# Splitting the final range checks of a list-scheduled attention kernel, moving them ahead of the last residual adds, and re-tuning the scheduler with it

## The chip, the cores and the metric

The kernel runs on one core of one Trainium2 chip. Time is device microseconds (us) of one execution of the whole program. Runs are only compared with runs of the same rounds on the same chip, unless the text says otherwise. e1 to e4 ran on one chip and e5 to e12 on another; the record doesn't name the chip of the comparison with the changed kernel. Engines: PE is TensorE (matmuls), PEld its weight loads, DVE is VectorE, ACT is ScalarE, POOL is GpSimd, SP is SyncE (transfers).

## The reference, cut to what matters

Four layers work on x of 2048 rows by 512 columns, in bf16: A, B, A, B, each as `x + f(layernorm(x))`. A is attention of 32 heads over eight dilated neighbours of each position. B is full attention in which 32 query heads share one key and value head, and it is most of the work:

```python
scores = jnp.einsum("bhqd,bkd->bhqk", q, k) * (Dh ** -0.5)   # 32 heads x 2048 x 2048
p = _softmax(scores, axis=-1)
o = jnp.einsum("bhqk,bkd->bhqd", p, v)
return o.transpose(0, 2, 1, 3).reshape(B, S, H * Dh) @ wo    # then x + this
...
x = A_x
x = x + _A_ref(_layernorm(x), ...)      # and B, and A, and B again
```

## The kernel before

The softmax is computed without subtracting a row's maximum. ScalarE takes some of the exponentials as a real `exp`; VectorE and GpSimd take the rest in pieces: VectorE copies a tile of scores out as 16-bit integers ("t"), and "passes" on integers then shift it ("i"), one on VectorE and others on GpSimd. This is only right while sums and reciprocals stay in range, so running sums (`chk_a`, `chk_b`, and two wide ones in the tile `oncA`) are compared with limits at the end: flags are made with `is_lt`, a minimum is taken, one matmul counts partitions that are good, and the verdict `chk_bad` decides whether a slow, safe program runs after all. In all runs here it doesn't.

The order of instructions on each engine is settled when the program is built, by a list scheduler with planned durations. It takes the candidate with the lowest key. Priorities are nanoseconds added to the planned start, so "LATER" is half a microsecond:

```python
AGE = 0.034
FIRST, SOON, LATER = -1000.0, -500.0, 500.0
SPAN, ACTIVE = 3413.0, 0.74
SLACK, PATIENCE = 798.0, 70.6
...
            if e in op.port:                      # VectorE/GpSimd work that declares `port`
                s = max(s, self.port)
            s = self.pe_start(op.mode, op.sub, s) if e == "pe" else max(s, self.now[e])
            if s < FAR:
                key = s + op.prio - AGE * (s - op.ready)
                if s + op.engs[e] + SWITCH > due + SLACK and s - op.ready < PATIENCE:
                    key = max(key, due + 1.0)
...
    def keep_awake(self, until):                  # called before each planned TensorE operation
        ...
        active = sum(b - max(a, old) for a, b in self.array_busy if b > a)
        t = min(gap, ACTIVE * SPAN - active)      # matmuls on zeros, if the plan is less busy than ACTIVE
```

The last block of the last layer ends in `close_tail(a, evac)`, called for its two halves a = 0 and 1. `evac` is VectorE's copy of a finished sum of attention products (`X <- o`); the copy of the second half ends the stream of attention tiles. Then come sums (`dn`), a logarithm and an exponential on ScalarE for reciprocals (`rec`), two normalisations on VectorE (`ons`), four output products, four residual adds and the checks:

```python
    def close_tail(self, a, evac):
        ...
        if a == 0:
            self.on0, self.seen = ons[0], sees
            return

        def most(op):       # five flags and one reduction of 1344 elements
            for i in self.checks.flag_most(self.i[0][:].rearrange("p r c -> p (r c)").bitcast(BF16)):
                self.chain("dve", i)

        y, adds = {}, []
        self.op("dve", 2300.0, most, [evac, *self.seen, *sees], prio=LATER)
        ...                 # four products begin, two to each score buffer
            m = self.op("pe", MM, end, [ons[qi // 2], begun[qi]], solid=True)
            adds.append(self.op("dve", 599.0, lambda op, qi=qi: self.add_y(l, qc, qi, y[qi]), [m], prio=SOON))

        def last(op):       # flag and minimum of the last reciprocals, count, chk_bad
            ...
        rec.used(self.op("dve", 1500.0, last, adds))
```

Of the kernel before, what the change touches and what calls it, by code (L numbers as in the profile page):

```python
# [435 lines left out]
SLACK, PATIENCE = 798.0, 70.6  # L436
# [179 lines left out]
class Stream:  # L616

    GROUP = 4
    BIAS = {"act": -50.0, "act2": 1946.7, "vec": 438.1, "pv": 246.6, "pv_in": 177.5, "batch": 17, "few": 19.9,
            "copy": 1.6, "pass": 76.2, "lag": -1045.1, "both": 216.8, "next": 634.6, "late": 31.8, "open": 54.2,  # L620
# [217 lines left out]
class Checks:  # L838
# [4 lines left out]
    def __init__(self, nc, pool):  # L843
        self.nc, self.pool = nc, pool
        self.a = pool.tile([128, 256], F32, name="chk_a")
        self.b = pool.tile([128, 2, 32], F32, name="chk_b")
        self.t = None
        self.blank = [nc.vector.memset(x[:], 0.0) for x in (self.a, self.b)]
# [12 lines left out]
    def flag_most(self, ok):  # L861
        nc, v = self.nc, self.nc.vector
        self.ok, self.mb = ok, self.pool.tile([128, 2], BF16, name="chk_mb")
        out = [v.tensor_scalar(out=ok[:, at:at + n], in0=x, scalar1=lim, scalar2=None, op0=ALU.is_lt)
               for at, n, x, lim in ((0, 256, self.a[:], self.LOG_A ** 2), (256, 32, self.b[:, 0, :], self.SUM_B),
                                     (288, 32, self.b[:, 1, :], self.REC_B), (320, 512, self.t[:, 0, :], self.SUM_B),
                                     (832, 512, self.t[:, 1, :], self.REC_B))]
        return [*out, v.tensor_reduce(out=self.mb[:, 0:1], in_=ok[:, 0:1344], axis=AX.X, op=ALU.min)]

    def flag_last(self, recips):  # L870
        v, ok = self.nc.vector, self.ok[:, 1344:1856]
        return [v.tensor_scalar(out=ok, in0=recips, scalar1=self.REC_B, scalar2=None, op0=ALU.is_lt),
                v.tensor_reduce(out=self.mb[:, 1:2], in_=ok, axis=AX.X, op=ALU.min)]

    def count(self, cnt):
        self.bad = self.pool.tile([1, 1], I32, name="chk_bad")
        return (self.nc.tensor.matmul(cnt[:], lhsT=self.mb[:, 0:1], rhs=self.mb[:, 1:2], start=True, stop=True),
                self.nc.vector.tensor_scalar(out=self.bad[:], in0=cnt[:], scalar1=127.5, scalar2=None, op0=ALU.is_lt))
# [60 lines left out]
class Net:  # L939
# [180 lines left out]
    def mm_full(self, pairs, deps, name):  # L1120
# [17 lines left out]
        b = self.op("pe", half * MM, rest, behind=[a], solid=True, prio=-2724.2 + self.PRIO)  # L1138
# [3 lines left out]
    def ln(self, B, src, deps, after=(0.0,) * 4, quick=False, own=None):  # L1142
# [6 lines left out]
        for i in range(4):  # L1149
            def emit(op, i=i):  # L1150
                self.chain("dve", nc.vector.bn_stats(out=stats[:, i, :], in_=src(i)))

            st.append(sm.used(self.op("dve", 596.0, emit, [*deps[i], *sm.prev], prio=-84.0 + self.PRIO, after=after[i])))
# [13 lines left out]
        for some in ((0, 1), (2, 3)) if quick else ((0, 1, 2, 3),):  # L1167
            ag = sm.used(self.op("dve", 70.0 * len(some), lambda op, some=some: aggr(op, some), [st[i] for i in some],
                                 prio=-1808.0 + self.PRIO))
            ag = sm.used(self.op("pool", 1700.0, lambda op, some=some: scalars(op, some), [ag], prio=899.8 + self.PRIO))  # L1170
            nm.update(dict.fromkeys(some, ag))
        B.xnT.renew()
        xnT, done = B.xnT.t, []
        for i in range(4):
# [14 lines left out]
            if quick:  # L1189
                def turn(op, xn=xn):  # L1190
                    pT = self.psum(op, [128, 4, 128], BF16, "pT")
                    for ft in range(4):
# [4 lines left out]
                                     prio=-3069.4 + self.PRIO))  # L1197
                tr = self.op({"act": act_ns(512), "dve": 400.0}, 0, lambda op, cols=cols, tr=tr: self.chain(
                    op.eng, (nc.scalar.copy if op.eng == "act" else nc.vector.tensor_copy)(
                        out=cols, in_=self.y.pop(tr)[:])), [tr], frees=[tr], prio=74.1 + self.PRIO)  # L1200
            else:
                tr = xn.used(self.op("sp", 1300.0, lambda op, cols=cols, xn=xn: self.chain(
                    "sp", nc.sync.dma_start_transpose(out=cols, in_=xn.t[:])), [n, *B.xnT.prev], prio=-2301.2 + self.PRIO))
# [49 lines left out]
    def qkv(self, B, c, xops, quick):  # L1253
# [20 lines left out]
        def split(op):  # L1274
            for g in range(4):
                for h in range(2):
# [6 lines left out]
                                                                  prio=932.5 + self.PRIO)))]] * 4  # L1283
# [3 lines left out]
        for k2 in range(4):  # L1287
# [14 lines left out]
            m = self.op("pe", 450.0, lambda op, mm=mm: mm(op, i=1), behind=[m0], solid=True, mode="h64", prio=-703.1 + self.PRIO)  # L1302
# [21 lines left out]
    def unit(self, B, c, t, kd, qkv):  # L1324
# [38 lines left out]
        ms = P.used(self.op("dve", 800.0, mask, exps, prio=-609.7 + self.PRIO, port=("dve",)))  # L1363
# [31 lines left out]
        p1 = self.op("pe", 165.0, lambda op: pv(op, 1), behind=[p0], solid=True, mode="c64", prio=-2478.1 + self.PRIO)  # L1395
        m = self.op("pe", 250.0, dn, behind=[p1], solid=True, mode="c64", prio=-1502.3 + self.PRIO)
        m.lend = p0
        for x in (p0, p1, m):
# [5 lines left out]
            out=lg.t[:], in_=state["o"][:, 1, :], func=AF.Ln)), [m, *lg.prev], prio=-145.2 + self.PRIO))  # L1404
        ex = lg.used(rc.used(self.op("act", act_ns(256), lambda op: self.chain("act", nc.scalar.activation(  # L1405
            out=rc.t[:], in_=lg.t[:], func=AF.Exp, scale=-1.0)), [ln, *rc.prev], prio=-68.5 + self.PRIO)))
        if t == 0 and kd == 0:
# [3 lines left out]
            [ex, *B.oncA.prev], frees=[m], prio=-227.8 + self.PRIO)))  # L1411
# [6 lines left out]
        lg.used(self.op("pool", 1400.0, see, [ex], prio=1246.8, port=("pool",)))  # L1418
        return on

    def a_out(self, B, l, c, units):
        nc, adds = self.nc, []
        for qi in range(4):
# [7 lines left out]
                prio=-24.6 + self.PRIO))  # L1431
        return adds

    def b_in(self, B, l, c, adds):
# [18 lines left out]
        v = B.xnT.used(self.op("pe", 400.0, mm, xops + self.padded[l], want=("bank", "aux"), solid=True, prio=190.0 + self.PRIO))  # L1453
# [80 lines left out]
    def rows(self, l, qc, t, a, evac):  # L1534
# [43 lines left out]
        r = R2.used(S2.used(self.op("dve", 260.0, recip, [m, self.ready[l, qc, t, 0], *R2.prev], prio=-25.5)))  # L1578
        R2.used(S2.used(self.op("pool", 620.0, see, [r], prio=27.1)))
        d = R2.used(self.op("sp", 2 * DMA, to_dram, [r]))  # L1580
        b = lb.used(self.op("sp", DMA, spread, [d, *lb.prev]))
        if t == 0:
            self.oncB.renew()
        self.ready[l, qc, t] = self.oncB.used(lb.used(X0.used(
            self.op("pool", 1300.0, scale, [b, m, *self.oncB.prev], prio=3120.3, port=("pool",)))))
# [7 lines left out]
    def out_rows(self, l, qc, qi):  # L1593
        m = self.oncB.used(self.mm_full([(self.oncB.t[:, t, qi * 128:(qi + 1) * 128], self.w.woB[:, t, :])
                                         for t in range(4)], [self.ready[l, qc, t] for t in range(4)], "y"))
        return self.op("dve", 599.0, lambda op: self.add_y(l, qc, qi, self.y.pop(m)[:]), [m], frees=[m], prio=-35.1)

    def retire_w(self):
# [7 lines left out]
        z = self.op("pool", 960.0, lambda op: self.chain("pool", nc.gpsimd.memset(w.woP, 0.0)), done, prio=256.3)  # L1606

        def load(op):
            for g in range(4):
# [5 lines left out]
                             self.oncA.cur, prio=6302.3)  # L1615
# [14 lines left out]
    def close_tail(self, a, evac):  # L1630
# [15 lines left out]
        for cs, dn in zip(parts, dns):  # L1646
# [8 lines left out]
        sees = [rec.used(self.op("pool", 1300.0, lambda op, n=n, x=x: self.chain("pool", self.checks.see_wide(n, x.t[:])),  # L1655
                                 [after, self.wiped])) for n, x, after in ((0, X, evac), (1, rec, re))[:2 - a]]
        if a == 0:
            self.on0, self.seen = ons[0], sees
            return

        def most(op):
            for i in self.checks.flag_most(self.i[0][:].rearrange("p r c -> p (r c)").bitcast(BF16)):
                self.chain("dve", i)

        y, adds = {}, []
        self.op("dve", 2300.0, most, [evac, *self.seen, *sees], prio=LATER)
        begun = []
        for qi in range(4):
            def start(op, qi=qi):
                if qi % 2 == 0:  # L1670
# [3 lines left out]
                for k in range(4):  # L1674
# [5 lines left out]
            b = self.op("pe", 4 * MM, start, deps, want=("slot", "y") if qi % 2 == 0 else None, solid=True,  # L1680
                        behind=[begun[-1]] if qi % 2 else [])
            begun.append(b)
        for qi in range(4):
# [6 lines left out]
            adds.append(self.op("dve", 599.0, lambda op, qi=qi: self.add_y(l, qc, qi, y[qi]), [m], prio=SOON))  # L1690

        def last(op):
            for i in self.checks.flag_last(rec.t[:]):
# [210 lines left out]
```

## Time and profile before

| | before |
|---|---|
| time, first three runs | 1502.85 us median |
| time, six runs beside the changed kernel | 1502.40 us median (1500.34 to 1505.17) |
| profiled execution | span 1500.2 us, mean granted TensorE clock 0.994 |
| evacuation of the last block's first half ends | 1468.48 us |
| last evacuation ends | 1485.32 us: the last block takes 16.83 us |
| end | 14.85 us after that |

This is the timeline of the kernel before (start, us, engine, line, operation, out<-in, sizes, and in brackets the idle time before it and who ended it).

```profile
1481.22 1.71 DVE L1495 TENSOR_SCALAR i<-t 128x1024 int16<-128x1024 int16 x1
...
1483.10 1.04 POOL L1490 TENSOR_TENSOR i<-t,off 128x512 int32<-128x512 int32 x1 [0.46 <-DVE i L1495]
...
1484.62 0.69 DVE L1523 COPY X<-o 128x512 f32<-128x512 f32 x1 [1.69 <-PE o L1507]
```

The last VectorE pass releases the last GpSimd pass, which releases the last attention product, for which the evacuation waits 1.69 us. Whatever delays that VectorE pass delays the end, even though VectorE is idle after it.

### The profile page before, as it was taken

How to read it: one execution, taken by the hardware profiler on the slowest of the kernel's cores; microseconds unless marked ns; L12 is line 12 of the kernel's file. 1: busy time of each engine (PE TensorE's matmuls, PEld its weight loads, DVE VectorE, ACT ScalarE, POOL GpSimd, SP SyncE). 2: the span in 40 equal slices, each digit the busy share in tenths (PEclk: the TensorE clock that was granted, in tenths of full speed). 3: DMA queues.
4: the chain of work that ended last, by engine and by line, in shares of the span. 5: the costliest groups of instructions: out<-in, count | busy, mean ns of one | idle time of the engine just before them, and what ended most of it. 6: DMA issues, size and time to landing. Idle time of an engine off the chain costs nothing.

```text
span 1500.2 us, 42220 instructions
## 1 busy us (share of the span) xinstructions
PE 1430.8 (95%) x17204; PEld 494.9 (33%) x17263; DVE 1339.5 (89%) x2301; ACT 1437.1 (96%) x1754; POOL 896.9 (60%) x741
## 2 busy tenths in 40 slices
PE   8899999999999999999999999999999999999996
PEld 4534343223422233222333224322222222222222
DVE  5787868998799978999789997899999999999997
ACT  6899999999999999999999999999999999999995
POOL 3745546565566656666575664757566656665664
PEclk9999999999999999999999999999999999999999
DMA  4010110011010020100201001001000000000000
GB/s 142 5 29 3 30 16 16 17 31 34 14 23 13 17 38 7 27 13 16 35 13 27 13 15 16 16 9 43 27 12 14 13 23 17 9 18 20 16 9 24
DMA packets 84114, 32.95 MB, mean 22 GB/s; under 512 B 71688, under 2 KB 77448, under 8 KB 83912
## 3 DMA queue, kind: packets, MB, share of 16 engines
q1 hardware_dynamic: 83048, 28.33, 8.8%
q8 instruction: 137, 2.24, 0.6%
q10 hardware_dynamic: 864, 1.84, 0.3%
q14 instruction: 65, 0.53, 0.1%
HBM read 13.53 MB, written 2.61 MB: 11 GB/s over the span
## 4 chain that ended last, share of the span: by engine, by line
ACT 45%; PE 42%; issue 7%; DVE 4%; POOL 1%; DMA 0%; ACTq 0%; POOLq 0%; DVEq 0%
ACT pt L1481 40%; PE o L1507 14%; PE st L1466 14%; PE y L1130 3%; ACT P L1353 2%; PE q L1130 2%; PE k L1130 2%; PE qb L1130 2%; DVE t L1485 2%; PE v L1297 1%; PE dv L1466 1%; ACT logs L1403 1%; ACT rec L1405 1%; PE st L1346 1%; DVE i L1495 1%
## 5 line engine op out<-in xcount | busy, mean ns | idle before, releaser
L1481 ACT ACTIVATE pt<-st 128x1024 bf16<-128x1024 f32 x1359 | 1271.8, 1168 | 16.9 <-PE o L1507 9.1
L1490 POOL TENSOR_TENSOR i<-t,off 128x1024 int32<-128x1024 int32 x345 | 656.2, 1904 | 488.1 <-DVE i L1495 332.7
L1485 DVE TENSOR_SCALAR t<-dv 128x512 int16<-128x512 f32 x1378 | 877.9, 683 | 51.3 <-PE dv L1466 41.5
L1466 PE MATMUL st<-QT,KAB 32*128 32x512 bf16 x1388 | 270.4, 381 | 13.4 <-ACT pt L1481 8.1
L1466 PE MATMUL st<-QT,region 32*128 32x512 bf16 x1330 | 259.1, 379 | 18.4 <-ACT pt L1481 13.9
L1507 PE MATMUL o<-pt,region 128*32 128x512 bf16 x1330 | 270.7, 386 | 0.2
L1507 PE MATMUL o<-i,region 128*32 128x512 f16 x1436 | 265.3, 385 | 1.0 <-DVE i L1495 0.7
L1507 PE MATMUL o<-pt,VEa 128*32 128x512 bf16 x1388 | 261.0, 386 | 0.4 <-DVE x_sb L1429 0.4
L1495 DVE TENSOR_SCALAR i<-t 128x2048 int16<-128x2048 int16 x345 | 238.6, 695 | 3.9 <-PE o L1507 3.1
L1507 PE MATMUL o<-i,VEd 128*32 128x512 f16 x1320 | 240.4, 385 | 0.8 <-POOL i L1490 0.7
L1466 PE MATMUL dv<-QT,region 32*128 32x512 bf16 x718 | 231.5, 382 | 1.0 <-DVE t L1485 1.0
L1466 PE MATMUL dv<-QT,KAB 32*128 32x512 bf16 x660 | 214.6, 383 | 0.0
L1507 PE MATMUL o<-t,region 128*32 128x512 f16 x718 | 181.5, 385 | 0.2 <-DVE t L1485 0.2
L1466 PEld LDWEIGHTS <-region 32*128 32x128 bf16 x2048 | 95.5, 90 | 259.6 <-issue 255.2
L1466 PEld LDWEIGHTS <-KAB 32*128 32x128 bf16 x2048 | 90.7, 90 | 264.4 <-issue 258.0
L1507 PE MATMUL o<-t,VEd 128*32 128x512 f16 x660 | 173.7, 385 | 0.6 <-issue 0.6
L1507 PEld LDWEIGHTS <-region 128*32 128x32 f16 (+1 forms) x3484 | 73.8, 94 | 162.4 <-issue 158.3
L1353 ACT ACTIVATE P<-st 128x576 bf16<-128x576 f32 (+1 forms) x128 | 89.6, 726 | 3.4 <-PE st L1346 3.3
L1507 PEld LDWEIGHTS <-VEd 128*32 128x32 f16 x1980 | 64.4, 94 | 72.6 <-issue 67.7
L1507 PEld LDWEIGHTS <-VEa 128*32 128x32 bf16 x1388 | 58.1, 94 | 79.6 <-issue 77.7
L1360 DVE TENSOR_TENSOR P<-P,bandmask 128x576 int32<-128x576 int32 x64 | 59.0, 926 | 28.3 <-ACT P L1353 26.1
L1414 POOL TENSOR_TENSOR logs<-logs 128x256 f32<-128x256 f32 x64 | 47.5, 742 | 30.2 <-ACT rec L1405 30.2
(173 smaller groups left out, 1180.3 us busy)
## 6 DMA issues: line engine op xcount, KB each, us to landing
lb<-rd SPq DMA_DIRECT2D x31, 256.0 KB
X<-X SPq DMA_DIRECT2D x124, 32.0 KB
k<-oncA SPq DMA_DIRECT2D x48, 64.0 KB
w_sb<-in_A_wqkv_dram ACTq DMA_DIRECT2D x4, 384.0 KB
region<-in_A_x_dram SPq DMA_DIRECT2D x3, 512.0 KB
out_dram<-w_sb SPq DMA_DIRECT2D x3, 512.0 KB
S<-X SPq DMA_DIRECT2D x62, 8.0 KB
rd<-R SPq DMA_DIRECT2D x62, 8.0 KB
```

The lines of the kernel that those rows point to most:

```text
L1130: self.chain("pe", self.nc.tensor.matmul(st["ps"][:], lhsT=lhsT, rhs=rhs, start=first and n == 0, stop=last and n == len(some) - 1))
L1297: self.chain("pe", nc.tensor.matmul(ps[0][64 * a:64 * a + 64, i], lhsT=B.xnT.t[:, kt, kb * 64:(kb + 1) * 64], rhs=wv[:, kt, a, :, :], star ...
L1346: self.chain("pe", nc.tensor.matmul(st[:, j, col:col + w], lhsT=kx[gs], rhs=qt[gs, qbase + q0:qbase + q0 + w], start=True, stop=True, tile ...
L1353: "act", nc.scalar.activation(out=P.t[:, gh, :, c0:UC], in_=self.st.pop(sc)[:, :, c0:UC], func=AF.Exp, scale=DH ** -0.5)), [sc], frees=[sc ...
L1360: self.chain("dve", nc.vector.tensor_tensor(out=x, in0=x, in1=self.w.band[:].unsqueeze(1).to_broadcast([128, 16, NQ // 2]), op=ALU.bitwise ...
L1414: self.chain("pool", nc.gpsimd.tensor_tensor(out=lg.t[:], in0=lg.t[:], in1=lg.t[:], op=ALU.mult))
L1466: self.chain("pe", self.nc.tensor.matmul(out, lhsT=self.KAB[l][32 * g:32 * g + 32, a, kt * 128:(kt + 1) * 128], rhs=self.QT[32 * g:32 * g ...
L1481: self.chain("act", self.nc.scalar.activation(out=self.pt[pt][:, 0:n, :], in_=self.st.pop(key)[:, 0:n, :], func=AF.Exp, scale=E_SCALE))
L1485: self.chain("dve", self.nc.vector.tensor_scalar(out=self.t[buf][:, r, :].bitcast(I16), in0=self.dv[bank][:], scalar1=-U_BIAS, scalar2=U_B ...
L1490: i = self.nc.gpsimd.tensor_tensor(out=self.i[out][:, 0:n, :].bitcast(I32), in0=self.t[buf][:, 0:n, :].bitcast(I32), in1=self.w.off[j][:, ...
L1495: i = self.nc.vector.tensor_scalar(out=self.i[out][:, 0:n, :].bitcast(I16), in0=self.t[buf][:, 0:n, :].bitcast(I16), scalar1=J_OFF[j], sca ...
L1507: self.chain("pe", self.nc.tensor.matmul(self.o[bank][32 * g:32 * g + 32, :], lhsT=lhsT, rhs=rhs, start=first, stop=last, tile_position=(0 ...
```

## The change

The intent is to take the checks off the end. The flags of what is known early, and their minimum in two halves, may run as soon as the first half of the last block has closed; the flag of X itself replaces a GpSimd addition; the flag of the last reciprocals goes ahead of the adds; only `chk_bad` stays behind them. The first of the four output products begins in a bank of its own. 34 constants of the scheduler move along: 25 priorities, seven biases, SLACK and PATIENCE (the prediction's "about 25" counts the priorities alone). The core of the diff, cut (line numbers of helpers shift by four):

```diff
-SLACK, PATIENCE = 798.0, 70.6
+SLACK, PATIENCE = 1876.6, 16.6
...
-    BIAS = {"act": -50.0, "act2": 1946.7, "vec": 438.1, ... "pass": 76.2, "lag": -1045.1, "both": 216.8, ...
+    BIAS = {"act": -50.3, "act2": 972.8, "vec": 438.1, ... "pass": 74.1, "lag": -1287.5, "both": -37.6, ...
...            (25 priorities, two of them here)
-            ag = sm.used(self.op("pool", 1700.0, ..., [ag], prio=899.8 + self.PRIO))
+            ag = sm.used(self.op("pool", 1700.0, ..., [ag], prio=1268.0 + self.PRIO))
...
-                    "sp", nc.sync.dma_start_transpose(out=cols, in_=xn.t[:])), [n, *B.xnT.prev], prio=-2301.2 + self.PRIO))
+                    "sp", nc.sync.dma_start_transpose(out=cols, in_=xn.t[:])), [n, *B.xnT.prev], prio=-3570.1 + self.PRIO))
...            (close_tail, a == 0)
+            small = self.op("dve", 560.0, lambda op: chain(
+                chk.flag(ok[:, 0:256], chk.a[:], chk.LOG_A ** 2), chk.flag(ok[:, 256:288], chk.b[:, 0, :], chk.SUM_B),
+                chk.flag(ok[:, 288:320], chk.b[:, 1, :], chk.REC_B)), [*chk.seen, *self.xnT.cur], prio=LATER)
+            wide = [self.op("dve", 360.0, lambda op, n=n, lim=lim: chain(
+                chk.flag(ok[:, 320 + 512 * n:832 + 512 * n], chk.t[:, n, :], lim)), [seen[n], *self.xnT.cur], prio=LATER)
+                for n, lim in ((0, chk.SUM_B), (1, chk.REC_B))]
+            half = self.op("dve", 800.0, lambda op: chain(chk.all_of(ok[:, 1344:1345], ok[:, 0:672])), [small, *wide],
+                           prio=LATER)
+            self.most = self.op("dve", 800.0, lambda op: chain(chk.all_of(chk.mb[:, 0:1], ok[:, 672:1345])), [half],
+                                prio=LATER)
...            (a == 1)
-        self.op("dve", 2300.0, most, [evac, *self.seen, *sees], prio=LATER)
+        own = self.op("dve", 1050.0, lambda op: chain(chk.flag(ok[:, 1345:1857], X.t[:], chk.SUM_B),
+                                                      chk.all_of(ok[:, 512:513], ok[:, 1345:1857])), [evac, self.most])
+        mine = rec.used(self.op("dve", 1050.0, lambda op: chain(
+            chk.flag(ok[:, 0:512], rec.t[:], chk.REC_B), chk.all_of(chk.mb[:, 1:2], ok[:, 0:513])), [re, own, *ons],
+            prio=FIRST))
+        n = self.op("pe", 60.0, ... chk.count(...), [mine], want=("bank", "aux"), solid=True)
+        self.op("dve", 140.0, ... chk.over(self.y[n]) ..., [n], frees=[n], prio=SOON)
...
-                if qi % 2 == 0:
+                if qi == 0:
+                    y[0] = self.psum(op, [128, 512], name="y")[:]
+                elif qi != 2:
...
-        rec.used(self.op("dve", 1500.0, last, adds))
```

## The prediction

> **What bounds the kernel now.** I read the page's busy line and chain first, to learn which engines share the bound.
>
> ```profile
> PE 1430.8 (95%) x17204; PEld 494.9 (33%) x17263; DVE 1339.5 (89%) x2301; ACT 1437.1 (96%) x1754; POOL 896.9 (60%) x741
> ...
> ACT 45%; PE 42%; issue 7%; DVE 4%; POOL 1%; DMA 0%; ACTq 0%; POOLq 0%; DVEq 0%
> ```
>
> ScalarE and TensorE carry 87% of the chain between them and both are full; VectorE is close behind. For about 1,470 us this is a stream of attention tiles whose exponentials are divided between ScalarE and VectorE by a list scheduler that runs when the kernel is built. The change's named part isn't there but at the end, so I cut the last 20 us into stretches (start:end, length, then busy us and count for PE, weight loads, DVE, ACT and POOL).
>
> ```profile
> 1482.90:1484.60 1.70, 1.40 (x14) 0.62 (x10) 0.03 (x1) 0.19 (x1) 1.04 (x1) 1.00 0.01 5
> 1484.60:1487.30 2.70, 2.65 (x12) 1.49 (x14) 0.73 (x2) 1.15 (x4) 1.26 (x1) 1.00 0.00 0
> 1487.30:1490.60 3.30, 2.65 (x13) 0.98 (x10) 3.27 (x9) 0.23 (x1) 0.00 (x0) 1.00 0.00 0
> 1490.60:1494.50 3.90, 0.16 (x1) 0.08 (x1) 3.61 (x8) 0.00 (x0) 0.00 (x0) 0.90 0.39 134
> 1494.50:1500.20 5.70, 0.00 (x0) 0.00 (x0) 0.00 (x0) 0.00 (x0) 0.00 (x0) 0.50 0.05 11
> ```
>
> VectorE (third number) is idle for 1.7 us before 1484.6, while everyone waits for one last GpSimd pass, and for about 2 us more after that, and then alone sets the end from 1487.3 to 1494.5. After that nothing computes for 5.7 us. The chain of waits says what VectorE does there (start, us, what):
>
> ```profile
> 1487.26 0.76 DVE w_sb L1652 x2
> 1488.02 1.05 DVE i L864 x5
> 1489.07 0.02 issue
> 1489.10 1.56 DVE chk_mb L868
> 1490.65 2.38 DVE w_sb L1623 x4
> 1493.04 0.35 DVE i L872
> 1493.39 0.02 issue
> 1493.41 0.70 DVE chk_mb L873
> 1494.11 0.04 issue
> 1494.15 0.18 PE chk_cnt L877
> 1494.33 0.02 issue
> 1494.35 0.15 DVE chk_bad L878
> ```
>
> L864 to L878 are the range checks. The first half (1.05 + 1.56 us) stands between the last normalisation (L1652) and the four residual adds (L1623), the second half (0.35 + 0.70 + 0.18 + 0.15 us) behind the adds. All of it is on the path. What comes after is seen in the instructions of the final branch:
>
> ```profile
> L1872 PEldq COMPARE_BRANCH  x1: 3967/3967/3967, 1495.1 to 1495.1; - x1
> ...
> L1872 DVEq EVENT_SEMAPHORE  x1: 21/21/21, 1498.1 to 1498.1; - x1
> ```
>
> Every engine loads the verdict (chk_bad) at 1494.53, and branches over the unused slow program at 1495.1. TensorE's branch takes 3.97 us. The end is then chk_bad + 5.7 us (1494.50 to 1500.2). VectorE's own leg is shorter: it passes its branch at 1498.1, 3.6 us after chk_bad, and the closing barrier behind the last engine takes some 1.0 us (1499.2 to 1500.2), so about 4.7 us.
>
> [...] 1556 ns for 1344 elements and 689 ns for 512 is (1556 - 689) / 832 = 1.04 ns an element[...]; so cutting a reduction in two costs only one more fixed part, 689 - 512 x 1.04 = 156 ns. [...] three engines' branches are followed by instruction packets of 16 KB in all each, the last landing at 1499.24, just where TensorE goes on. [...] the 1024-element pass at 1481.22 took 1.71 us beside a GpSimd add that ran to 1482.65, where one twice as wide takes 0.68 us otherwise. [...] In the trace before, the last matmul (1489.96) precedes the first add (1490.57)[...].
>
> **The change part by part.**
>
> 1. Flags of what is known early (1.05 us for the five: chk_a, chk_b twice, and the wide sums twice) and their minimum, now in two halves of 672 and 673 elements, each about 673 x 1.04 + 156 = 857 ns, so 1.71 instead of 1.56 us. They're released some 10 us before the last block closes, at the lowest priority. Off the path: 1.05 + 1.56 = 2.61 us. They need 2.8 us of VectorE in the last block. The gap at 1482.9 holds 1.7 of that; the rest falls into the 1.94 us wait for ScalarE (1485.31 to 1487.26) or pushes a tile of the stream over to ScalarE, which has 3.0 us idle there. I charge 0.3 us.
> 2. "own": flag and minimum of X itself (0.36 + 0.69 = 1.05 us), in place of a GpSimd addition (1.26 us at 1485.39, off the path). Fits the 1.94 us wait: 0.
> 3. "mine": flag and minimum of the last reciprocals, 0.36 + 0.69 = 1.05 us, now ahead of the adds at top priority. Start 1488.02 + 0.06, end 1489.14.
> 4. The adds may then begin, if TensorE has the products. It starts its last four matmuls at 1488.93 in the trace before; the first is readable near 1489.36 (one takes 0.38 us, and I allow 0.05 for the signal). So TensorE replaces VectorE's checks as what releases the first add: 1489.4 instead of 1490.57, and the last add ends at 1489.4 + (1493.04 - 1490.57) = 1491.9 instead of 1493.04. Gain 1.15 us.
> 5. Behind the adds only chk_bad is left. Its count (one matmul) is ready near 1490.2. By the scheduler's rule (equal priority, the oldest ready goes first) I expect it after all four adds: 1491.9 to 1492.05. Then 1492.05 + 5.7 = 1497.75, a gain of 2.45 us. If it slips between the adds, TensorE's long branch starts under them, and VectorE's leg decides: 1492.05 + 4.7 = 1496.7, a gain of 3.5 us.
> 6. One product in its own bank: both kernels create these operations only when the last block closes, when both score buffers are already free (the last exponential ended at 1483.1, the first product began at 1484.5). Worth 0 by itself; it saves at most the wait for the second buffer in a schedule where ScalarE finishes last.
> 7. About 25 scheduler constants move. "lag" (negative before and after, compared with a difference that can't be negative) and with it "both", and "next" (634 or 869 against at most 64 outstanding tiles) are never effective. "act2" is halved (TensorE fills the second score buffer sooner) and SLACK/PATIENCE nearly stop projections being held back for the stream. This re-orders all 1,480 us. From the trace I can bound it: ScalarE idles 63 us in all, of which 14 in the first 40 us, 16 up to 240 us and about 14 behind 1485; the 19 us left over the middle, and some of the start, are what a better order can win. A re-tuning made together with the edit is more likely to help than to hurt; I put 2.5 us on it, give or take 5. This is a guess within that bound, not a sum.
>
> Sum: -2.45 (or -3.5) for the tail, +0.3, -2.5 for the order: about -4.8 us, 1502.85 - 4.85 = 1498.0.
>
> **Rivals.** (a) The tail gain is lost: the 2.8 us of checks delay the last VectorE and GpSimd passes, which gate the last products (the chain from 1472 to 1484 is VectorE passes, one GpSimd pass, then TensorE). For it: VectorE is 97% busy from 1420 to 1470. Against: the priority is 500 ns below all stream work, and the idle 1.7 us. It would leave about 1501 with the order's part zero. (b) The schedule's change dominates: in 1,480 us a new order can be worth +6 or -10 us, and then the tail is a detail; 1492 to 1506. For: both main engines are on the chain with hundreds of short waits, so small shifts add up; against: ScalarE is already 98 to 100% busy from 240 to 1470 us. (c) The output transfer takes over as the end: the last transfer landed at 1494.43, 1.4 us behind its add, so it would land at 1493.3, long before 1497; it stays hidden.
>
> **Range and chances.** The tail is good to about 1 us, the order to about 5 us, so 8 in 10 lies within 1490 to 1503.5. Two per cent is 30 us, half of all of ScalarE's idle time; 0.02 for faster, 0.01 for slower.
>
> **What would show it.** Chain: no flags between L1652 and the adds but one pair; the adds start within 1.5 us of the last normalisation's end (before: 2.55); chk_bad last or among the adds; last add to end of the span 5.9 us or less (before 7.2). ScalarE's idle time in the middle falls if the order helped. What would make it wrong: the last product of the stream ends more than 5 us away from 1484.6 less 2.5 (the order's part mis-sized), or the checks sit in the chain ahead of the last evacuation (rival a).

Its sum came to about -4.8 us (4.85 in its last line), which gives 1498.0. The 1.04 ns an element and the 156 ns of a reduction come from its two measured reductions alone. The 0.06 and 0.05 us allowed for a start and for a signal in steps 3 and 4 were estimates of mine, made by hand; in the trace before, the last evacuation (1484.62) starts 0.04 us behind the end of the products that it waits for (1484.19 + 0.39), and `chk_bad` 0.02 us behind its count.

## More of the kernel before

The new early checks declare no `port`; the stream's VectorE passes do. `port` is a word of the scheduler: what declares it, on VectorE or GpSimd, is planned one after the other.

## The result, and the profile after

The changed kernel took 1506.53 us (median of six runs, 1505.95 to 1509.27), against 1502.40 us before. A ratio in this document is the mean time of one kernel's fast runs over that of the other's of the same rounds (in the experiments without the first, profiled run of each), so it isn't quite the ratio of the medians quoted: here 1.0032, with a 95% interval of 1.0018 to 1.0047. That is within 2%, as expected, but on the wrong side: I predicted 1498.0, and 1490 to 1503.5.

The busy line and the shares of the chain, from the page of the changed kernel:

```profile
PE 1433.0 (95%) x17213; PEld 494.2 (33%) x17274; DVE 1350.0 (90%) x2316; ACT 1435.0 (95%) x1748; POOL 894.0 (59%) x738
...
PE 43%; ACT 43%; issue 7%; DVE 6%; POOL 1%; ACTq 0%; POOLq 0%; DVEq 0%
```

VectorE is 10.5 us busier than before, with fifteen instructions more, and its share of the chain rose from 4% to 6%. The end of the changed kernel in stretches (start:end, length, then busy us and count for PE, weight loads, DVE, ACT and POOL, granted clock, DMA share, GB/s):

```profile
1485.90:1489.70 3.80, 2.69 (x20) 0.89 (x17) 3.77 (x6) 0.84 (x1) 1.54 (x1) 1.00 0.02 4
1489.70:1491.70 2.00, 1.28 (x8) 0.48 (x9) 0.34 (x2) 0.00 (x0) 1.04 (x1) 1.00 0.00 0
...
1496.40:1499.10 2.70, 0.76 (x5) 0.18 (x2) 2.59 (x5) 0.00 (x0) 0.00 (x0) 1.00 0.28 96
1499.10:1504.80 5.70, 0.00 (x0) 0.00 (x0) 0.00 (x0) 0.00 (x0) 0.00 (x0) 0.78 0.19 59
```

The stretch in which VectorE alone set the end (3.3 and 3.9 us before) is down to the 2.7 us of the adds. But there is a new one: from 1485.9 VectorE is full for 3.8 us, and then everything waits 2 us for a short VectorE pass and one GpSimd pass. The chain of waits of the changed kernel names what filled it (start, us, what):

```profile
1485.38 0.60 DVE t L1481
1485.98 2.08 DVE xnT L864 x2
1488.06 0.77 DVE xnT L867
...
1488.85 0.86 DVE chk_mb L867
1489.71 0.34 DVE i L1491
...
1490.21 1.05 POOL i L1486
...
1491.30 0.39 PE o L1503 x2
...
1496.45 2.53 DVE w_sb L1619 x4
1498.98 0.06 DVE chk_bad L874
```

L864 and L867 are the flags and reductions of the early checks. The last tile of scores was copied out at 1485.98. Two flags and two reductions then ran until 1489.71, 3.73 us, and only after them the tile's VectorE pass, which releases GpSimd's. The checks are in the chain ahead of the last evacuation: that is rival (a) of the prediction. The end of the chain is as intended: no reduction stands between the adds and `chk_bad`.

Some of these flags took far longer than their size says. The timeline of VectorE and that of GpSimd, changed kernel, at the same moments:

```profile
1471.34 2.01 DVE L864 TENSOR_SCALAR xnT<-chk_a 128x256 bf16<-128x256 f32 x1
1473.27 1.33 DVE L864 TENSOR_SCALAR xnT<-chk_b 128x32 bf16<-128x32 f32 x2
```

```profile
1471.31 1.89 POOL L1486 TENSOR_TENSOR i<-t,off 128x1024 int32<-128x1024 int32 x1
1473.16 1.32 POOL L861 TENSOR_TENSOR oncA<-oncA,lb 128x512 f32<-128x512 f32 x1
```

VectorE starts these flags just after a GpSimd instruction has started, and they end just after it: 1471.31 + 1.89 = 1473.20, where the flag of `chk_a` ends at 1473.35; 1473.16 + 1.32 = 1474.48, where the two flags of `chk_b` end at 1474.60. Of two flags in a row it is the first that is long: those of `chk_b` took 1.24 and 0.17 us, those of `oncA` 1.82 and 0.41. So here a flag of 32 elements (1.24 us) lasted about as long as what GpSimd had in hand (1.32 us). Together the five early flags took 2.01 + 1.33 + 2.16 (`oncA`, twice) = 5.5 us; the plan had 560 + 2 x 360 ns for them, 1.28 us.

Where the 4.64 us of the two profiled spans come from, by the two evacuations:

| us | before | changed | difference |
|---|---|---|---|
| evacuation of the last block's first half ends | 1468.48 | 1469.63 | +1.15 |
| last block, until the last evacuation | 16.83 | 22.80 | +5.97 |
| from there to the end | 14.85 | 12.39 | -2.46 |
| span | 1500.17 | 1504.81 | +4.64 |

A difference of 1.15 us at 1469 hides more than it shows. In stretches of 3.41 us the granted clock of TensorE falls to 0.50. Up to 1470 us the kernel before had 10.2 us at half clock (53 to 60, 115 to 118), the changed one 17.1 us (11 to 14, 58 to 62, 116 to 120, 253 to 260). Evacuation by evacuation the changed kernel falls 0.97 us behind at the first of these and is still so at 247 us; after 253 to 260 it is 3.73 us behind; by 1468 it has recovered 2.6 us of that at full clock. The low stretches in these traces, but for those that the end of a run cuts off, last 3.41, 6.83, 10.24, 13.65 and (once, in e11) 17.07 us, one to five times the shortest.

### The profile page after: what moved, and what is told of

The parts are those of the page before. It is cut to its first block, busy times and chain, and to the rows that moved or that the text cites. A ratio compares the mean times of both kernels' runs of the same rounds, so it can differ in the third digit from the quotient of the medians.

```text
span 1504.8 us, 42245 instructions
## 1 busy us (share of the span) xinstructions
PE 1433.0 (95%) x17213; PEld 494.2 (33%) x17274; DVE 1350.0 (90%) x2316; ACT 1435.0 (95%) x1748; POOL 894.0 (59%) x738
## 3 DMA queue, kind: packets, MB, share of 16 engines
q10 hardware_dynamic: 864, 1.84, 0.3%
## 4 chain that ended last, share of the span: by engine, by line
PE 43%; ACT 43%; issue 7%; DVE 6%; POOL 1%; ACTq 0%; POOLq 0%; DVEq 0%
ACT pt L1477 38%; PE o L1503 15%; PE st L1462 14%; PE y L1126 3%; DVE t L1481 3%; ACT P L1349 2%; PE q L1126 2%; PE k L1126 2%; PE qb L1126 2%; PE dv L1462 1%; PE v L1293 1%; ACT logs L1399 1%; DVE i L1491 1%; PE st L1342 1%; ACT rec L1401 1%
## 5 line engine op out<-in xcount | busy, mean ns | idle before, releaser
L1462 PE MATMUL st<-QT,KAB 32*128 32x512 bf16 x1384 | 270.4, 383 | 14.9 <-ACT pt L1477 10.4
L1503 PE MATMUL o<-pt,region 128*32 128x512 bf16 x1330 | 275.9, 386 | 0.1
L1503 PE MATMUL o<-pt,VEa 128*32 128x512 bf16 x1384 | 264.1, 389 | 0.4 <-DVE x_sb L1425 0.4
L1503 PE MATMUL o<-i,VEd 128*32 128x512 f16 x1328 | 247.9, 387 | 0.7 <-POOL i L1486 0.6
L1491 DVE TENSOR_SCALAR i<-t 128x2048 int16<-128x2048 int16 x346 | 235.5, 683 | 0.5
```

What stands on the lines that cost most here:

```text
L1462: self.chain("pe", self.nc.tensor.matmul(out, lhsT=self.KAB[l][32 * g:32 * g + 32, a, kt * 128:(kt + 1) * 128], rhs=self.QT[32 * g:32 * g ...
L1491: i = self.nc.vector.tensor_scalar(out=self.i[out][:, 0:n, :].bitcast(I16), in0=self.t[buf][:, 0:n, :].bitcast(I16), scalar1=J_OFF[j], sca ...
L1503: self.chain("pe", self.nc.tensor.matmul(self.o[bank][32 * g:32 * g + 32, :], lhsT=lhsT, rhs=rhs, start=first, stop=last, tile_position=(0 ...
```

## The experiments

After the result there were three explanations, which don't exclude each other. The first (checks): the early checks hold up the last passes, and so cost more than the tail gains. The second (constants, or order): the re-tuned constants give an order that is slower in itself. The third (clock): the new order, or chance, gets less clock from the throttle. (That low activity of TensorE is what lowers it, as the expectations of e7, e9 and e10 have it, was a supposition to be tested.)

Two tools serve all runs. The first is the sum "last block + tail" of a profile, from the end of the first half's last evacuation to the end of the span (the expectations of e1 to e4 count the tail from the last attention product, 0.7 us earlier: their 15.6 and 13.1 us are 14.9 and 12.4 here); it is free of the clock's history in the stream (no such stretch fell into the last block). The second separates clock from schedule: over 110 runs of all fourteen kernels, on all chips together, I fitted time = a level for each kernel + one common slope times the run's mean granted clock (which is recorded in thousandths). The slope is 1.04 us (give or take 0.03) for each thousandth, or 0.69 us for each us of clock lost in 1,502, with a scatter of 0.8 us. "Level" below is a kernel's fitted time at clock 0.995 less that of the kernel before, good to some 0.35 us. "Clock" is the mean granted clock less that of the kernel before in the same rounds, in thousandths; its standard error is 0.8 to 2.5 for one row, so a single row shows little.

| kernel | median us (before) | ratio, 95% interval | clock | level | last block + tail |
|---|---|---|---|---|---|
| before | 1502.40 | | | 0 | 16.83 + 14.85 = 31.68 |
| changed | 1506.53 (1502.40) | 1.0032 [1.0018, 1.0047] | mean 0.9915 | +1.8 | 22.80 + 12.39 = 35.19 |
| e1 structure, old constants | 1502.21 (1502.36) | 0.9990 [0.9970, 1.0011] | +1.8 | +0.55 | 19.25 + 12.45 = 31.70 |
| e2 constants, old structure | 1505.92 (1502.36) | 1.0024 [0.9995, 1.0053] | -3.8 | -0.3 | 19.50 + 14.87 = 34.37 |
| e3 checks after the last evacuation | 1505.78 (1502.36) | 1.0023 [1.0001, 1.0046] | -2.1 | +0.7 | 19.50 + 15.40 = 34.90 |
| e4 checks port-aware | 1505.31 (1502.36) | 1.0010 [0.9987, 1.0033] | -4.1 | -1.9 | 18.74 + 12.36 = 31.10 |
| e5 old constants, GpSimd flags | 1503.59 (1504.69) | 0.9996 [0.9973, 1.0019] | +0.9 | 0.0 | 18.67 + 12.12 = 30.79 |
| e6 old constants, no own bank | 1504.76 (1504.69) | 1.0006 [0.9987, 1.0026] | +0.9 | +1.3 | 19.24 + 12.79 = 32.03 |
| e7 priorities only | 1509.86 (1504.69) | 1.0056 [1.0024, 1.0088] | -3.9 | +3.5 | 18.33 + 14.99 = 33.32 |
| e8 SLACK, PATIENCE only | 1502.81 (1504.69) | 0.9987 [0.9969, 1.0005] | +0.6 | -0.3 | 17.27 + 14.48 = 31.75 |
| e9 changed, more idle matmuls | 1506.75 (1505.37) | 1.0012 [0.9989, 1.0035] | +1.8 | +3.3 | 22.80 + 12.04 = 34.84 |
| e10 before, more idle matmuls | 1505.72 (1505.37) | 1.0012 [0.9984, 1.0039] | -0.2 | +1.3 | 16.84 + 14.99 = 31.83 |
| e11 port-aware, more idle matmuls | 1504.25 (1505.37) | 0.9985 [0.9959, 1.0012] | +1.0 | +0.2 | 18.84 + 12.38 = 31.22 |
| e12 old constants, port-aware | 1501.07 (1505.37) | 0.9973 [0.9952, 0.9993] | +2.5 | -0.8 | 17.76 + 12.38 = 30.14 |

All outputs are right. A comparison of the built programs' instruction orders, with line numbers left aside, helps to read the table. In before, e1, e5, e6, e8 and e12 the order is the same on every engine up to the last block; in the changed kernel, e2, e3 and e4 it is likewise one and the same order up to there. So within each of these two families the first 1,465 us are the same program. Yet e1, e5, e6, e8 and e12, whose stream is that of before, had between 0.6 and 2.5 thousandths more clock than before in their rounds: so much chance alone can do.

### e1: the new structure with the old constants

```diff
 # the changed kernel, with every constant as before
-SLACK, PATIENCE = 1876.6, 16.6
+SLACK, PATIENCE = 798.0, 70.6
 # ... and BIAS and all priorities likewise
```

> The changed structure with every scheduler constant of the kernel before. Theory A (checks inside the last block: low-priority flags issued beside GpSimd work are held by it, and flags and reductions stand ahead of the last VectorE pass): the last block, from the evacuation of its first half (X, second last) to that of the last, is 4 to 6 us longer than the 16.8 us of before, the tail behind the last product is 2.5 us shorter (13.1 against 15.6), together 1504.5 to 1506. Theory B (the new constants lost the time, the structure is good): the last block keeps its 16.8 us and the time is 1502.4 - 2.5 = 1500.

Measured: ratio 0.9990, the last evacuation 2.75 us later than in before (1488.07 against 1485.32, with the same half-clock stretches ahead of it), the tail 2.4 us shorter. The structure by itself gives back what it gains: 31.70 us from the first half's evacuation to the end, against 31.68. So theory A had the place right, but the loss in the block is 2.42 us and not 4 to 6; theory B's 1500 didn't come. Here too the checks stand between the last copy of scores (ends near 1481.6) and the pass that it needs (1485.27): two flags of 2.16 us together, then 0.84 and 0.86 us of reductions. Of the 2.42 us, 0.10 arise up to the end of that copy and 2.32 behind it. There the first flag (1.83 us) only takes the place of the pass: in before the pass itself took 1.71 us, beside a GpSimd pass that ran to 1482.65, and in e1 it took 0.42. What makes the pass late is what still comes ahead of it, the second flag (0.41) and the two reductions.

### e2: the new constants with the old structure

```diff
 # the kernel before, with every constant as in the changed one
-SLACK, PATIENCE = 798.0, 70.6
+SLACK, PATIENCE = 1876.6, 16.6
 # ... and BIAS and all priorities likewise
```

> The structure of before with all new constants. Theory A: the last block stays near 16.8 us, the tail stays 15.6 us, and the stretch from 505 to 1468 us is some 2.6 us shorter than before, so about 1500 (1498.5 to 1502). Theory B: the loss is here, 1506.5 + 2.5 = 1509, and the last block is some 6 us longer in this kernel too.

Measured: ratio 1.0024, clock 3.8 thousandths below that of before in the same rounds, which at 1.04 us each is 4.0 us. At equal clock the new order is worth -0.3 us: it isn't slower in itself, nor the 2.5 us faster that I had put on it. Its last block is 2.67 us longer (19.50 against 16.83), so by the fit it must gain about as much ahead of it. Both expectations failed: not 1500 us, nor 1509 with a block 6 us longer. In the profile, one stretch with the clock at half looks so (columns as above):

```profile
932.70:936.10 3.40, 2.01 (x72) 1.03 (x66) 3.23 (x4) 2.89 (x4) 3.32 (x3) 1.00 0.00 0
936.10:939.50 3.40, 3.40 (x116) 2.15 (x112) 0.88 (x2) 2.87 (x7) 1.54 (x3) 0.50 0.02 5
939.50:942.90 3.40, 3.40 (x32) 0.51 (x24) 2.87 (x5) 2.18 (x4) 1.34 (x2) 0.50 0.02 5
```

TensorE was busy for 2.01 of 3.40 us, and then ran two stretches of 3.40 us at 0.50. Behind the gap was a VectorE mask of layer A beside a GpSimd pass (1.88 us from 932.53): it took 2.15 us, where the mask before it (931.21) took 0.76, and a VectorE normalisation after it ended TensorE's longest wait, 1.22 us. `keep_awake` had put two matmuls on zeros ahead of that wait (0.30 and 0.27 us), and none into it; why the plan saw no more room wasn't traced.

### e3: the early checks only after the last evacuation

```diff
 # small, wide, half and most move from close_tail(0) to close_tail(1), and depend on the last evacuation:
-                chk.flag(ok[:, 288:320], chk.b[:, 1, :], chk.REC_B)), [*chk.seen, *self.xnT.cur], prio=LATER)
+                chk.flag(ok[:, 288:320], chk.b[:, 1, :], chk.REC_B)), [*chk.seen, *self.xnT.cur, evac], prio=LATER)
```

> The changed kernel, but the early flags and reductions also wait for the last evacuation, so that none of them stands in the last block. Theory A: the last block returns to about 16.8 us (-6), but the checks are on the path behind it again, tail 15.6 us or so (+2.5): about 1503. Theory B: the block stays long, 1506.5 to 1509.

Measured: the last block shrank from 22.80 to 19.50 us, just what e2 has without any early check, so the early checks cost the changed kernel 3.30 us there (expected were 6). Up to the end of the last copy of scores they cost 0.97 us, and 2.32 behind it, as in e1: the last pass took 1.71 us in e3 and 0.42 in the changed kernel, so again the second flag and the two reductions are what makes it late. Behind the evacuation the same flags are short, as the timeline of VectorE in e3 shows:

```profile
1485.59 0.28 DVE L864 TENSOR_SCALAR xnT<-chk_a 128x256 bf16<-128x256 f32 x1
1485.79 0.26 DVE L864 TENSOR_SCALAR xnT<-chk_b 128x32 bf16<-128x32 f32 x2
1485.96 0.75 DVE L864 TENSOR_SCALAR xnT<-oncA 128x512 bf16<-128x512 f32 x2
```

1.29 us in place of 5.5. (GpSimd wasn't looked at in e3; in the changed kernel its last instruction ends at 1491.25, ahead of the last evacuation, which starts at 1491.73.) But the tail is 15.40 us, longer than before the change, because the two reductions (0.85 and 0.86 us) are ahead of the adds again, and the flags and minima of X and of the last reciprocals (2.2 us) have gone behind them; so the time wasn't the 1503 of theory A. Moving the checks back isn't a cure; 34.90 is hardly less than 35.19.

### e4: the early checks declared as `port` work, and held back harder

```diff
-    ... [*chk.seen, *self.xnT.cur], prio=LATER)           # small; wide likewise
+    ... [*chk.seen, *self.xnT.cur], prio=-300.0, port=("dve",))
-    half = ... prio=LATER);  self.most = ... prio=LATER)
+    half = ... prio=1300.0); self.most = ... prio=1300.0)
```

> The changed kernel, but the scheduler is told that the early flags need the port [...] (so it places them where GpSimd rests), and the two early reductions come behind the last VectorE pass. Theory A: the flags take 1.3 us in all in place of 5.5 us, the reductions nothing; last block 1.5 us longer than 16.8 in place of 6.0, tail kept at 13.1 us: 1506.5 - 4.5 = 1502. Theory A without the port (only the position counts, not GpSimd): the flags keep 2 us each and little is won, 1505. Theory B: 1506.5.

Measured: the last block took 18.74 us in place of 22.80, with the tail as short (12.36). At equal clock e4 is 3.7 us below the changed kernel and 1.9 below before, the lowest level of all. In its runs that is lost again to the clock, 4.1 thousandths below before: ratio 1.0010. The flags of `chk_a` took 0.50 us and those of `chk_b` 0.25; one wide flag still took 1.49 us (from 1481.43, beside a GpSimd addition from 1480.87 to 1482.64), which the planned durations didn't foresee. The block came near theory A's 18.3 us; the time of 1502 didn't come. But e4 doesn't show which edit did it: the flags were shorter (2.65 us in all), the reductions came behind the last VectorE pass, and the scheduler also gave ScalarE 15 exponentials in the block instead of 14 and VectorE 14 copies of scores instead of 16. The block is even shorter than that of e3, which has no early checks in it, so part of the gain isn't the checks'.

### e5: the early flags on GpSimd

```diff
 # e1, with the flags on GpSimd in place of its additions to the wide sums:
-            seen = [... chk.see_wide(n, x.t[:]) ...]
-            small = self.op("dve", 560.0, ...);  wide = [self.op("dve", 360.0, ...) ...]
+            small = self.op("pool", 1400.0, ... nc.gpsimd.tensor_scalar(..., op0=ALU.is_lt) ..., port=("pool",))
+            wide = [rec.used(self.op("pool", 1000.0, ... nc.gpsimd.tensor_scalar(..., op0=ALU.is_lt) ..., port=("pool",))) ...]
-            half = ... prio=LATER);  self.most = ... prio=LATER)
+            half = ... prio=1300.0); self.most = ... prio=1300.0)
```

> The changed structure with the constants of before; the early flags are made on GpSimd (in place of its additions of the first half's sums), so VectorE has only the two early reductions, which the scheduler may put only where VectorE would wait over 1.3 us. If the 2.4 us that the last block lost in e1 came from flags that waited for GpSimd and stood ahead of the last pass: the time to the last evacuation falls by 2 to 2.7 us against e1 (1488.1 to about 1485.7 at the same clock), tail kept at 12.4 us behind that evacuation: 1502.2 - 2.4 = 1499.8, faster than the kernel before by 0.15%. If the loss is VectorE's extra work as such (two reductions, 1.7 us): 1501.5 to 1502.2.

Measured: ratio 0.9996. The last evacuation came at 1488.14 us, against 1488.07 in e1, but with 3.4 us more at half clock ahead of it. The last block, which is free of that, is 0.58 us shorter than e1's (18.67 against 19.25) and not 2 to 2.7, so the first expectation failed. The timeline of VectorE in e5 shows why:

```profile
1482.60 0.85 DVE L870 TENSOR_REDUCE xnT<-xnT 128x1 bf16<-128x672 bf16 x1
1483.48 0.86 DVE L870 TENSOR_REDUCE chk_mb<-xnT 128x1 bf16<-128x673 bf16 x1
1484.25 0.88 DVE L1494 TENSOR_SCALAR i<-t 128x1536 int16<-128x1536 int16 x1
```

The flags are gone from VectorE, but in spite of their priority of 1300 the two reductions still stand ahead of the last pass. This is the second expectation, VectorE's extra work as such, and its 1501.5 to 1502.2 us agree with the fit (1501.8 at clock 0.995). Nor were the flags free on GpSimd, which spent 0.87, 1.20, 1.49 and 1.81 us on them; what they cost there wasn't separated. (The sum of last block and tail is 0.9 us less than e1's; level 0.0 against +0.55.)

### e6: without a bank of its own

```diff
 # e1, products begun as in before: qi 0 and 1 in one score buffer, 2 and 3 in the other
-                if qi == 0:
-                    y[0] = self.psum(op, [128, 512], name="y")[:]
-                elif qi != 2:
+                if qi % 2 == 0:
```

> As e1 (changed structure, old constants), but all four last products begin in the score buffers as before. If the bank is worth nothing, as both score buffers are free by then: tail behind the last evacuation 12.4 us as in e1, 1502.2. If the bank saves a wait: up to 0.9 us (one product's four matmuls) longer tail, 1503.

Measured: tail 12.79 us against 12.45 in e1, everything ahead alike. The first adds in the timelines of e1 and e6, in this order:

```profile
1492.10 0.69 DVE L1619 TENSOR_TENSOR w_sb<-x_sb,y 128x512 bf16<-128x512 f32 x1 [0.27 <-PE y L1697]
```

```profile
1491.82 2.48 DVE L1619 TENSOR_TENSOR w_sb<-x_sb,st 128x512 bf16<-128x512 f32 x4 [0.70 <-PE st L1695]
```

In e1 the first add waits 0.27 us for its product, in e6 0.70 us. In e6 it starts 0.85 us after the first of the four last matmuls (1490.97), which is 0.04 us after the end of the third (one takes 0.38 us, all four 1.03, so they are 0.22 apart); in e1 it starts 0.42 us after the first (1491.68), 0.04 us after that one's end. So the bank's gain is 0.70 - 0.27 = 0.43 us of waiting, by an earlier start behind the matmuls, 0.34 us at the end.

### e7: only the new priorities

```diff
 # the kernel before, with the priorities of the changed one; BIAS, SLACK and PATIENCE as before
-                                     prio=-3069.4 + self.PRIO))
+                                     prio=-2853.9 + self.PRIO))
 # ... and all others
```

> The kernel before with the new priorities of operations alone (not the stream's biases, not SLACK and PATIENCE). If the new constants lose granted clock because their order leaves more 3.4 us stretches of low TensorE activity, and the priorities carry it: mean clock of the runs .990 to .992, half-clock stretches in most profiles, about 1504 to 1506. If it is one of the other groups: mean clock .994, 1502.

Measured: ratio 1.0056, the slowest of all, 3.5 us at equal clock and 3.9 thousandths less clock (0.988; the expectation had .990 to .992 and 1504 to 1506, and no loss at equal clock). The priorities carry the re-order and lose by themselves; BIAS, SLACK and PATIENCE win that back in e2 (-0.3). In e7 the stretch at half clock at 920.0 came after one in which TensorE was busy for 3.38 of 3.40 us, so a gap just ahead isn't what all such stretches have in common.

### e8: only SLACK and PATIENCE

```diff
 # the kernel before, with
-SLACK, PATIENCE = 798.0, 70.6
+SLACK, PATIENCE = 1876.6, 16.6
```

> The kernel before with SLACK and PATIENCE of the changed kernel alone. If this pair carries the loss of clock: mean clock .990 to .992, 1504 to 1506. If not: .994, 1502.

Measured: ratio 0.9987, level -0.3, which is inside the error, and no loss of clock (+0.6): the second expectation. By themselves the two constants change no order at all until the last block: under the old priorities they don't act in the stream.

### e9, e10, e11: more idle matmuls

```diff
 # in the changed kernel (e9), in the kernel before (e10), and in e4 (e11)
-SPAN, ACTIVE = 3413.0, 0.74
+SPAN, ACTIVE = 3413.0, 0.92
```

> The changed kernel with the scheduler's target for TensorE activity at 0.92 instead of 0.74: more matmuls on zeros in TensorE's gaps, nothing else but about one moved VectorE instruction in a hundred. If the lost granted clock of the changed kernel (mean .9915) comes from its stretches of low TensorE activity: mean clock .994 or above, and by the slope over all runs so far (0.67 us per us of clock lost) 2.5 us or more less: 1504 to 1505. If the clock is drawn by chance: .9915, 1506.5 or, for the added matmuls, more.

> The kernel before with the same target of 0.92. If low activity is the cause: mean clock from .993 to .995 or above, and 1 to 2 us less than the kernel before in the same rounds. If chance: the same clock and time as before, or up to 1 us more.

> e4 (new constants, [...] reductions behind the last pass) with the target of 0.92. Both repairs together: 1500.2 at a clock of .995 by the fit, so 1499.5 to 1501 if the clock comes to .995, faster than both kernels; 1505 if the clock stays at .990.

Measured: the ratios are 1.0012, 1.0012 and 0.9985. With matmuls on zeros wherever the plan is less than 92% busy, the new order seems to get as much clock as the old one: +1.8 (e9) and +1.0 (e11), where the four kernels with the new priorities and without these matmuls (e2, e3, e4, e7) had -2.1 to -4.1. Over all their runs that is +1.4 (standard error 0.9, 12 runs) against -3.5 (0.9, 24 runs), in other rounds and partly on another chip. The kernel before gains no clock (-0.2), which is what the expectation had for chance. The matmuls cost something at equal clock: e9 less the changed kernel 1.5 us, e10 less before 1.3, e11 less e4 2.1. So the clock that the new order loses can probably be bought back, for 1.5 to 2.1 us of time where it is worth some 4; it is still no better than an order that doesn't lose it. The times that were expected of low activity as the cause (1504 to 1505, 1 to 2 us less than before, 1499.5 to 1501) came in none of the three.

### e12: the old constants with port-aware checks

```diff
 # e1, with the edit of e4
-    ... prio=LATER)                         # small, wide
+    ... prio=-300.0, port=("dve",))
-    ... prio=LATER)                         # half, most
+    ... prio=1300.0)
```

> The changed structure with old constants (e1)[...]. If the 2.75 us that the last evacuation lost in e1 came from flags held by GpSimd ahead of the last pass: last evacuation some 1.5 to 2.5 us earlier than e1 at the same clock, time at clock .995 about 1500.5 against 1502.4 of e1 and 1502.0 of before. If it is the work as such: 1502.

Measured: 1501.07 us against 1505.37 for before in the same rounds, ratio 0.9973 with an interval of 0.9952 to 0.9993. It is below the kernel before, and that in turn is below the changed one. How much of it is the kernel's? Its stream is before's, instruction by instruction, up to the last block, so its 2.5 thousandths of clock (2.6 us) are most likely luck of those six runs. What is left is the level, -0.8 us, and the last block with its tail, 30.14 us against 31.68. So I count it as about a microsecond, not four; against before of its own rounds alone the level is -0.6, hardly clear of its error. The last block is 1.49 us shorter than e1's, near the 1.5 to 2.5 expected, but not as intended: the flags took 3.5 us in all (3.7 in e1), and the two reductions still stood ahead of the last pass (1486.34 to 1488.07). What changed is that the wide flags ran before the last copies of scores, and that ScalarE took 14 exponentials in the block instead of 13.

## Why the prediction was wrong, point by point

**Steps 2 to 5 (the tail) held.** From the last evacuation to the end the change won 2.46 us; the step said 2.45. This isn't two errors that cancel: up to the first add it won 1.22 us (step 4: 1.15), and from there 1.24 (step 5: 1.30). `chk_bad` came last, behind the adds. The adds began at 1496.45, 1.32 us after the last normalisation ended (1495.13), and waited for the products, as step 4 had it. From the last add (1498.98) to the end it was 5.8 us, and TensorE's final branch took 3.98 us (before: 3.97). (In the case that didn't arise, 3.6 + 1.0 is 4.6 and not 4.7.)

**Step 1 failed: "I charge 0.3 us."** The early checks cost 3.30 us in the last block of the changed kernel (22.80 against 19.50 in e3 and e2), and 2.42 with the old constants (e1: 19.25 against 16.83; by the clock 2.75 us). That is the whole gain of the tail: flags and reductions were in the path, ahead of the last VectorE pass. Three things in its working were wrong. It took the flags' durations from the tail of before, 1.05 us for five, where GpSimd is done (its last instruction there ends at 1486.65, the first flag starts at 1487.94); among the stream, where the flags that met a GpSimd instruction lasted until it ended (that of `chk_a` to 1473.35, beside one to 1473.20), they took 5.5 us (1.26 + 0.25 + 2.16 = 3.7 in e1). I had seen this in the trace before, on the pass of 1.71 us, and not applied it to flags. It filled gaps of VectorE as if work put there came for free; the gap at 1482.9 lay behind the last pass, and the checks went ahead of it; 2.32 us of the loss, in the changed kernel and in e1 alike, arise there, where the reductions alone are 1.7 us long. And it read a priority of +500 as below all the stream: by the key it is half a microsecond, minus 34 ns for each microsecond waited.

**Rival (a) was what happened.** It said that the tail's gain is lost to the last passes, and about 1501 is left if the order's part is zero; e1, which has the order of before, took 1502.21. In the changed kernel the loss is larger than the gain. The reason that I gave against it, the low priority, is the one that fell.

**Step 7 failed: "I put 2.5 us on it."** The order's worth at equal clock is -0.3 us (give or take 0.35; e2), not -2.5. The other side of it, which had no place in the sum, is the granted clock. In the rounds of e1 to e4, on one chip, the 18 runs of the new order had a mean of 0.9903, the 16 of the old order 0.9942; standard errors are 0.0009 and 0.0005. The 3.9 thousandths are 4.1 us at the fitted slope. Where: after 505 us none of the seven profiles of the old order has a stretch at half clock, and five of the seven of the new priorities have one or two. Thin stretches don't explain it: of the windows of 3.41 us, the length of the shortest low stretch, between 505 and 1000 us (slid by 0.1 us), 2.6 to 3.2% have TensorE less than 85% busy in the changed kernel, e2, e3 and e4, and 1.4 to 2.3% in before, e1, e5, e6, e8 and e12; but e7, which lost as much clock, has 1.8%, and e11, which lost none, 2.7%. So the loss is measured, and its mechanism is not shown.

For the comparison the sum then reads, as an estimate: 4.85 us of difference of the means, of which 1.8 are at equal clock (the level, read from the table), so 3.0 are left for the clock, which is 2.9 thousandths at 1.04 us each. The changed kernel's six runs had a mean of 0.9915.

**Step 6 was a little off: "Worth 0 by itself."** It is worth 0.43 us of waiting, and 0.34 us of the end (e6), not by a free buffer but by the first add's earlier start behind the matmuls.

**The other two rivals.** (b) was right that the schedule's part is as large as the tail's, by way of the clock rather than by short waits. (c) was right: the output's transfers stayed hidden: in the changed kernel the last landed at 1500.4, and the end is 1504.8.

**What stays open.** How the throttle decides isn't settled, nor why the new order gets less clock. How much of the early checks' cost is the flags' longer time beside GpSimd and how much the reductions' place isn't separated either: e5, with no flags on VectorE, still has a block 1.84 us longer than before, but with more work on GpSimd, and in e4 and e12 the division of the tiles changed too. The traces of e1 and of the changed kernel only show that behind the last copy a flag (1.83 and 1.82 us) takes the pass's place. That e2 isn't slower at equal clock although its last block is 2.7 us longer means that its stream gains about 3 us; which waits it saves wasn't traced. The fit puts the changed kernel 2.1 us (give or take 0.5) above e2, the profiles' last block and tail only 0.8 us; 1.3 us are unexplained. And flags that still took long (in e12 the two of `chk_b`, 1.35 us, and one of the wide ones, 1.49 us), and reductions ahead of the last pass in e5 and e12, may mean that there is more to be had than e12 has; that wasn't tried.

## What to carry to other kernels

Work that fills a gap must be costed where it will run, not where it ran: a short VectorE flag put beside GpSimd's long instructions lasted up to 2.01 us instead of 0.28, and 1.7 us of reductions ahead of the last pass delayed everything behind it. A scheduler has to be told of both, and a priority of +500, or even +1300 (e5, e12), didn't tell it. When an edit and a re-tuning come together, time them apart, and compare at equal granted clock: here a clock difference of 4 thousandths was as large as every other effect. A few microseconds in 1,500 that six runs show may be clock alone, also between programs with the same order.
